# Single PSUM banks in rings of two in place of two-bank tiles, and block sums added bank by bank

## The chip, the cores and the metric

One core of a Trainium2 chip runs the whole program. The metric is device time in microseconds (us) of one execution, the median of several runs. Engines are named as in the profile: PE is TensorE's matmul stream and PEld its weight loads, DVE is VectorE, ACT is ScalarE, POOL is GpSimd, SP issues DMAs.

## The reference

Three layers follow each other. Attention with a decaying state gives `x` of 1536 tokens by 512; a gated feed-forward layer follows; then a layer of 8 experts, weighted by a normalised gate.

```
state = gamma * state + k_t v_t^T ;  y_t = scale * q_t state          # retention, 2 x 8 heads, 768 steps, dim 64
h = x @ w_in ;  g = h * clip(h + 3, 0, 6) / 6 ;  x = g @ w_out        # FFN, 512 -> 2048 -> 512
P = exp(x @ w_gate) normalised 8 times over rows and columns          # gate, 1536 x 8
out = sum over e of P[:, e] * (relu(x @ w1[e]) @ w2[e])               # 8 experts, 512 -> 1024 -> 512
```

## The kernel before

Every matmul operand is split into a high and a low part, and three products (high x high, high x low, low x high) are summed in PSUM. PSUM has eight banks, and four tags share them: `s0` and `s1` are rings of two single-bank tiles; `r` and `y` are each one tile of two banks, made once (`wide`, line 76), and `bank("r")` or `bank("y")` hands out its two halves in turn. The order of instructions on each engine is the order in which the Python code is written (a manual schedule); waits are put in by the tile framework from what reads and writes each tile. Engines take their instructions in that order.

The stages, by the time in the profiled span:

- Attention (0 to 64 us): for each of 12 chunks `attend` writes a `y` half (L326, L332), ACT and DVE copy it out as a high and a low part (L341, L342).
- FFN (64 to 366 us): `stage_a` makes `h` (L361, 12 matmuls of 512 columns, bank `s0`), and `stage_b` adds into four accumulators (L388): 0 and 1 are `s1` tiles, named acc, and 2 and 3 are the two halves of `r`. Every 4 or 6 steps a group ends: after the last three matmuls of accumulator i, `finish` copies or adds it out (ACT L403, DVE L405), then the matmuls of i + 1 follow. There are nine group ends (3 weight groups x 3 blocks of tokens).
- Experts, first half of the tokens (366 to 1004 us): a "pair" i is one block product by seven matrix products (`pair`, `product`, L668: seven times six matmuls of 384 columns, banks `s0`, `s1`), with ACT copies (L700), DVE adds (L699) and DVE and ACT relu parts (L677, L678) between. Between its steps stand pieces of `outputs`: an output tile is four pieces of three matmuls of 512 columns (L870) into one `y` half, then one eviction that scales and adds it on DVE (L877, L879, L883). Three tiles go with each pair: 36 matmuls of L870 to 42 of L668. DVE and ACT also split and combine the next weights here (L514, L515, L519 to L525). Two pairs make one turn of the outer loop.
- Experts, second half (1004 to 1446 us): pairs alternate with `outputs2`, which walks through seven products a turn (`STEPS`). Each product has two halves d (L797, six matmuls of 384 columns, one bank each) and goes into the two banks of `r` or of `y`, in the order r, y, r, y, r, r, y. After both halves DVE adds the running sum of both banks to `c` (L808, 128x768; the first four by ACT, L805). `g_forms` makes the operands (L759, L514, L515).
- Last outputs (1446 to 1469 us): L830, L837 with `r` and `y` in turn.

Of the kernel before, what the change touches and what calls it, by code (L numbers as in the profile page):

```python
# [9 lines left out]
F32 = mybir.dt.float32  # L10
# [4 lines left out]
AF = mybir.ActivationFunctionType  # L15
ALU = mybir.AluOpType
# [4 lines left out]
P = 128  # L21
# [6 lines left out]
BLK = 512  # L28
# [8 lines left out]
SB = UT // 2  # L37
# [20 lines left out]
def kernel(  # L58
# [11 lines left out]
    nc = tc.nc  # L70
# [2 lines left out]


    ps_s = ctx.enter_context(tc.tile_pool(name="ps_s", bufs=2, space=PSUM))
    wide = {t: ps_s.tile([P, 2, BLK], F32, tag=t, name=t, bufs=1) for t in "ry"}
    turn = {"r": 0, "y": 0}

    def bank(tag, name="h"):

        if tag in wide:
            turn[tag] += 1
            return wide[tag][:, (turn[tag] - 1) % 2]
        return ps_s.tile([P, BLK], F32, tag=tag, name=name)

    by_pair = lambda t: t.rearrange("p (h i) -> p h i", h=NPAIR)
    dr = ctx.enter_context(tc.tile_pool(name="dr", bufs=1, space=bass.MemoryType.DRAM))
# [153 lines left out]
    def spread(tag, to, row):  # L241

        t = by_pair(bank(tag, "dm"))
        nc.tensor.matmul(
            t.rearrange("p h i -> p (h i)"), tab[:, to * P:(to + 1) * P], tab[:, TO + row * BLK:TO + (row + 1) * BLK],
            start=True, stop=True,
        )  # L250
        return t
# [39 lines left out]
    def scores(n):  # L291
        if n >= NCH:
            return
        t = [by_pair(bank(f"s{j}", "sc")) for j in range(2)]
        for p in range(NPAIR):
            for j in range(2):
                r = slice(j * D, (j + 1) * D)
                nc.tensor.matmul(t[j][:, p], qk_t[n][r, 1, p], qk_t[n][r, 0, p], start=True, stop=True)
        for j in range(2):
            a_t[n, j] = a = at2.tile([P, NPAIR, P], F32, tag="a", name="a", bufs=4)  # L300
            nc.vector.tensor_tensor(out=a, in0=t[j], in1=dmask[:, j], op=ALU.mult)

    def state(n):
        b, c = divmod(n, NCB)
        if c == NCB - 1:
            return
        if c == 0:
            acc_r[b] = by_pair(bank("r"))
        for p in range(NPAIR):
            cs = slice(p * P, (p + 1) * P)  # L310
            nc.tensor.matmul(
                acc_r[b][:, p], ks_t[n][:, cs], kv_t[n][:, 1, cs],
                start=(c == 0 and p == 0), stop=True, skip_group_check=True,
            )
        for j in range(2):
            r = slice(j * D, (j + 1) * D)
            nc.scalar.activation(out=rs[n % 2][r, :, r], in_=acc_r[b][r, :, r], func=AF.Copy)
# [272 lines left out]
    SFIRST, SLAST = NPR // 2, NIT // 2 - 1  # L590
# [100 lines left out]
            out=slot_t[i, f, j], in0=t, scalar=0.0, in1=pb_t[e][:, j * SB:(j + 1) * SB], op0=ALU.max, op1=ALU.mult  # L691
        )

    slot_t = {}

    def pair(i):

# [88 lines left out]
    def outputs2(n, formed, fetched):  # L786
        o = y2["c"]
        seen = set()
        for k, (m, tag, fresh, q) in enumerate(STEPS):
            x = wide[tag]  # L790
            w = form_t.pop((n, m))
            hi, lo = cuts[n][k]
            for d in range(2):
                ds = slice(d * P, (d + 1) * P)
                jobs = [(w[:, s, l, ds], g[:, s]) for s in range(2) for l, g in ((0, hi), (0, lo), (1, hi))]
                for a, (l, r) in enumerate(jobs):
                    nc.tensor.matmul(  # L797
                        x[:, d, 0:SB], l, r, start=(fresh and a == 0), stop=(a == 5), skip_group_check=True
                    )
                if d == 0:  # L800
                    next(formed, None)
                    next(fetched, None)
                    yield
            if n == SFIRST and q not in seen:
                nc.scalar.activation(out=o[:, q], in_=x[:, :, 0:SB], func=AF.Copy)  # L805
                seen.add(q)
            else:
                nc.vector.tensor_tensor(out=o[:, q], in0=x[:, :, 0:SB], in1=o[:, q], op=ALU.add)  # L808
            yield

    def last_forms(n):
        for j in range(2):
# [88 lines left out]
    with tc.manual_schedule():  # L901
# [107 lines left out]
        fetched = fetch2()  # L1009
        formed = itertools.chain(*(g_forms(n) for n in range(SFIRST, SLAST)), last_forms(SLAST))  # L1010
        outs2 = itertools.chain(*(outputs2(n, formed, fetched) for n in range(SFIRST, SLAST)))
        done2 = 0

# [126 lines left out]
```

## Time and profile before

| what | us |
| --- | --- |
| median of 3 runs (1468.65 to 1476.88) | 1470.24 |
| the profiled execution's own time | 1470.33 |
| its span, first to last instruction | 1468.6 |
| PE busy / PEld busy | 1350.5 / 1198.1 |
| DVE busy | 986.2 |
| ACT busy | 529.5 |

The profiled execution is 0.1 us over the median; 1.7 us lie outside its span. PE is busy for 92% of the span, but a matmul's busy time overlaps the next one's, so what PE loses is read from its waits and from start to start. DVE's 67% is a mean over stages that differ much.

### The profile page before, as it was taken

What the parts mean: (1) busy time and instruction counts of PE and PEld (TensorE: products, weight loads), DVE (VectorE), ACT (ScalarE), POOL (GpSimd) and SP (SyncE); (2) the same over time, 40 slices, a digit from 0 to 9 for tenths busy, and PEclk for the clock granted to TensorE, in tenths of its full rate; (3) what the DMA queues carried; (4) which work ended last, traced back from release to release, by engine and by line L of the source; (5) the groups of instructions that cost most, each with busy time, mean ns of one, the idle gap of its engine ahead of it and who ended that gap; (6) DMA issues with size and microseconds to landing.
All of it is one profiled execution on the core that took longest, in us unless ns stands there. A gap on an engine that the chain in (4) does not pass through costs nothing.

```text
span 1468.6 us, 18041 instructions
## 1 busy us (share of the span) xinstructions
PE 1350.5 (92%) x7005; PEld 1198.1 (82%) x7005; DVE 986.2 (67%) x1615; ACT 529.5 (36%) x803; POOL 149.6 (10%) x223
## 2 busy tenths in 40 slices
PE   8989999998897888888888888999999999999998
PEld 7877777776776777777777777789999999999998
DVE  5866556336678766666666666566777877787773
ACT  4556434223442333333333333323323232322221
POOL 3300000000211222212222111100000000000000
PEclk8999999999999999999999999999999999999999
DMA  8522111002776677666767667759677676767661
GB/s 273 207 82 87 59 56 58 0 0 82 277 262 233 240 247 249 251 253 249 252 245 251 245 245 251 265 219 287 246 262 260 241 272 223 283 246 257 246 225 44
DMA packets 66641, 302.23 MB, mean 206 GB/s; under 512 B 7782, under 2 KB 13942, under 8 KB 58364
## 3 DMA queue, kind: packets, MB, share of 16 engines
q1 hardware_dynamic: 45020, 183.60, 35.7%
q0 software_dynamic: 21536, 117.48, 22.0%
q8 instruction: 55, 0.90, 0.2%
q14 instruction: 30, 0.25, 0.1%
HBM read 182.01 MB, written 119.04 MB: 205 GB/s over the span
## 4 chain that ended last, share of the span: by engine, by line
PE 64%; DVE 19%; ACT 8%; issue 2%; DMA 2%; POOL 0%; ACTq 0%; DVEq 0%
PE h L668 23%; PE y L870 9%; PE r L797 9%; PE h L361 8%; PE y L797 6%; PE r L388 4%; DVE o L883 4%; PE acc L388 3%; DVE w L515 3%; ACT w L514 2%; DVE st L515 2%; DVE g L678 2%; ACT st L514 2%; DMA kept<-w 1%; ACT g L677 1%
## 5 line engine op out<-in xcount | busy, mean ns | idle before, releaser
L668 PE MATMUL h<-xh,w 128*128 128x384 f32 x1792 | 528.6, 339 | 6.6 <-ACT t L700 4.8
L870 PE MATMUL y<-w,g 128*128 128x512 f32 x1152 | 316.4, 401 | 73.8 <-DVE o L883 60.5
L668 PEld LDWEIGHTS h<-xh,w 128*128 128x128 f32 x1792 | 332.0, 189 | 17.5 <-ACT t L700 5.8
L870 PEld LDWEIGHTS y<-w,g 128*128 128x128 f32 x1152 | 207.7, 189 | 132.2 <-DVE o L883 90.7
L668 PE MATMUL h<-xl,w 128*128 128x384 f32 x896 | 303.4, 339 | 0.0
L668 PEld LDWEIGHTS h<-xl,w 128*128 128x128 f32 x896 | 169.6, 189 | 9.8
L797 PE MATMUL r<-gh,w 128*128 128x384 f32 x480 | 141.4, 340 | 0.0
L514 ACT ACTIVATE gh<-g 128x768 fp32r<-128x768 f32 x64 | 54.2, 847 | 169.4 <-DVE g L759 89.8
L797 PE MATMUL y<-gh,w 128*128 128x384 f32 x360 | 106.7, 337 | 0.0
L883 DVE SCALAR_TENSOR_TENSOR o<-y,pm,o 128x512 f32<-128x512 f32 x84 | 62.6, 745 | 53.8 <-PE y L870 53.8
L797 PEld LDWEIGHTS r<-gh,w 128*128 128x128 f32 x480 | 88.2, 188 | 4.9 <-DVE c L808 4.9
L368 DVE SCALAR_TENSOR_TENSOR t<-t,h 128x512 f32<-128x512 f32 x48 | 33.0, 687 | 85.0 <-ACT t L366 84.3
L700 ACT ACTIVATE g<-h 128x384 f32<-128x384 f32 x96 | 45.1, 485 | 112.8 <-PE h L668 112.8
L515 DVE TENSOR_TENSOR w<-raw,w 128x1024 fp32r<-128x1024 f32 (+1 forms) x64 | 69.5, 1086 | 18.5 <-ACT w L514 18.5
L797 PE MATMUL r<-gl,w 128*128 128x384 f32 x240 | 80.6, 336 | 0.0
L538 POOL DMA_DIRECT2D kept<-w x32 | 17.8, 557 | 612.1 <-DVE w L515 612.1
L361 PE MATMUL h<-xhi,whi 128*128 128x512 f32 x192 | 78.5, 409 | 0.0
L361 PE MATMUL h<-xlo,whi 128*128 128x512 f32 x192 | 77.9, 406 | 0.0
L361 PE MATMUL h<-xhi,wlo 128*128 128x512 f32 x192 | 77.3, 402 | 0.3 <-DVE wlo L149 0.3
L515 DVE TENSOR_TENSOR gl<-t,gh 128x768 fp32r<-128x768 f32 x45 | 43.1, 959 | 44.4 <-ACT gh L514 44.4
L515 DVE TENSOR_TENSOR gl<-g,gh 128x768 fp32r<-128x768 f32 x64 | 60.9, 951 | 17.7 <-ACT gh L514 17.7
L366 ACT ACTIVATE t<-h,three 128x512 f32<-128x512 f32 x48 | 33.0, 687 | 92.8 <-PE h L361 91.0
(163 smaller groups left out, 2184.7 us busy)
## 6 DMA issues: line engine op xcount, KB each, us to landing
kept<-w POOLq DMA_DIRECT2D x32, 1792.0 KB, 6.3
w<-kept SPq DMA_DIRECT2D x32, 1792.0 KB, 9.3
w<-kept SPq DMA_DIRECT2D x105, 512.0 KB, 5.6
raw<-in_we SPq DMA_DIRECT2D x64, 512.0 KB, 4.2
kept<-st POOLq DMA_DIRECT2D x30, 1024.0 KB, 6.5
raw<-in_wf SPq DMA_DIRECT2D x32, 512.0 KB, 3.7
kept<-w POOLq DMA_DIRECT2D x60, 256.0 KB, 6.7
kept<-w POOLq DMA_DIRECT2D x60, 128.0 KB, 6.1
```

Source lines behind the costliest of these rows:

```text
L361: nc.tensor.matmul(h, w[:, ks], x[:, k], start=(n == 0), stop=(n == 3 * KT - 1))
L366: nc.scalar.activation(out=t, in_=h, func=AF.Relu, bias=three, scale=1.0)
L368: nc.vector.scalar_tensor_tensor(out=t, in0=t, scalar=6.0, in1=h, op0=ALU.min, op1=ALU.mult)
L388: nc.tensor.matmul(acc_b[i], l, r, start=(f == 0 and j == 0), stop=(f == nf - 1 and j == 2))
L514: nc.scalar.activation(out=hi, in_=t, func=AF.Copy)
L515: nc.vector.tensor_tensor(out=lo, in0=t, in1=f32(hi), op=ALU.subtract)
L668: nc.tensor.matmul(bank[:, 0:SB], l[:, w, ks], r[:, k], start=(start and n == 0), stop=(stop and n == 5), skip_group_check=True,)
L678: nc.vector.scalar_tensor_tensor(out=lo, in0=t, scalar=0.0, in1=f32(hi), op0=ALU.max, op1=ALU.subtract)
L700: copy = lambda out, a: nc.scalar.activation(out=out, in_=a, func=AF.Copy)
L797: nc.tensor.matmul(x[:, d, 0:SB], l, r, start=(fresh and a == 0), stop=(a == 5), skip_group_check=True)
L870: nc.tensor.matmul(acc, l[:, cs], r[:, f % 2], start=(f == 0 and k == 0), stop=(f == 3 and k == 2))
L883: nc.vector.scalar_tensor_tensor(out=o[:, tt], in0=acc, scalar=sc, in1=o[:, tt], op0=ALU.mult, op1=ALU.add)
```

## The change

`r` and `y` are no longer two-bank tiles: every `bank(tag)` call now makes a new single-bank tile from a ring of two per tag. Banks per tag stay at two, eight in all. In `outputs2` the two banks of `r` and the two of `y` are taken once, at its first turn, and each half d is added to `c` right after its own six matmuls: two DVE additions of 128x384 where one of 128x768 stood (and 8 ACT copies for 4). Matmuls, their order and all DMAs stay the same. Line numbers below the edit shift by -7 up to `pair`, -6 to -5 behind.

```diff
-    wide = {t: ps_s.tile([P, 2, BLK], F32, tag=t, name=t, bufs=1) for t in "ry"}
-    turn = {"r": 0, "y": 0}
-
-    def bank(tag, name="h"):
-
-        if tag in wide:
-            turn[tag] += 1
-            return wide[tag][:, (turn[tag] - 1) % 2]
-        return ps_s.tile([P, BLK], F32, tag=tag, name=name)
+    def bank(tag, name=None):
+        return ps_s.tile([P, BLK], F32, tag=tag, name=name or tag)
...
-            x = wide[tag]
+            if k < 2 and n == SFIRST:
+                sum_t[tag] = [bank(tag, name="acc") for d in range(2)]
+            x = sum_t[tag]
...
                     nc.tensor.matmul(
-                        x[:, d, 0:SB], l, r, start=(fresh and a == 0), stop=(a == 5), skip_group_check=True
+                        x[d][:, 0:SB], l, r, start=(fresh and a == 0), stop=(a == 5), skip_group_check=True
                     )
                 if d == 0:
                     next(formed, None)
                     next(fetched, None)
-                    yield
-            if n == SFIRST and q not in seen:
-                nc.scalar.activation(out=o[:, q], in_=x[:, :, 0:SB], func=AF.Copy)
-                seen.add(q)
-            else:
-                nc.vector.tensor_tensor(out=o[:, q], in0=x[:, :, 0:SB], in1=o[:, q], op=ALU.add)
-            yield
+                if n == SFIRST and (q, d) not in seen:
+                    nc.scalar.activation(out=o[:, q, d], in_=x[d][:, 0:SB], func=AF.Copy)
+                    seen.add((q, d))
+                else:
+                    nc.vector.tensor_tensor(out=o[:, q, d], in0=x[d][:, 0:SB], in1=o[:, q, d], op=ALU.add)
+                yield
```

Three places show what it does to the instruction streams. The first is PE in `outputs`, experts' first half, where one output tile ends and the next begins (`y_59` is the two-bank tile; an entry in brackets is the engine whose semaphore the instruction waits for). Before:

```order
L870 MATMUL y_59<-w2_5144,g_5172 128x512
L870 MATMUL y_59<-w2_5145,g_5172 128x512
L870 MATMUL y_59<-w2_5144,g_5172 128x512
L870 MATMUL y_59<-w2_5006,g_5065 128x512 [waits DVE_49]
L870 MATMUL y_59<-w2_5007,g_5065 128x512
L870 MATMUL y_59<-w2_5006,g_5065 128x512
```

The same place of the change, on PE (tiles `y_5607` and `y_5644` of the ring):

```order
L864 MATMUL y_5607<-w2_5529,g_5591 128x512
L864 MATMUL y_5607<-w2_5530,g_5591 128x512
L864 MATMUL y_5607<-w2_5529,g_5591 128x512 [waits DVE_49]
L864 MATMUL y_5644<-w2_5388,g_5374 128x512 [waits DVE_49]
L864 MATMUL y_5644<-w2_5389,g_5374 128x512
L864 MATMUL y_5644<-w2_5388,g_5374 128x512
```

Nothing moves. The wait of the next tile's first matmul was for DVE's eviction of the tile just finished, the other half of `y_59`; it is now for the eviction of the tile two back, which held the same bank. The new wait in the third row is for a low part of the operand (L671), which the earlier wait on DVE had covered.

The second place is PE at the end of a group in the FFN, the last three matmuls of accumulators 2 and 3. Before:

```order
L388 MATMUL r_58<-ghi_834,whi_696 128x512
L388 MATMUL r_58<-glo_835,whi_696 128x512
L388 MATMUL r_58<-ghi_834,wlo_697 128x512
L388 MATMUL r_58<-ghi_834,whi_696 128x512 [waits Activation_49]
L388 MATMUL r_58<-glo_835,whi_696 128x512
L388 MATMUL r_58<-ghi_834,wlo_697 128x512
```

And with the change:

```order
L381 MATMUL acc_821<-ghi_856,whi_716 128x512
L381 MATMUL acc_821<-glo_857,whi_716 128x512
L381 MATMUL acc_821<-ghi_856,wlo_717 128x512
L381 MATMUL acc_822<-ghi_856,whi_716 128x512
L381 MATMUL acc_822<-glo_857,whi_716 128x512
L381 MATMUL acc_822<-ghi_856,wlo_717 128x512
```

The wait of accumulator 3 for the eviction of accumulator 2 is gone.

The third place is DVE in `outputs2`, around one product of `STEPS`. Before:

```order
L690 SCALAR_TENSOR_TENSOR g<-h,pb 128x384
L759 TENSOR_TENSOR g<-g 128x768
L515 TENSOR_TENSOR gl<-g,gh 128x768 [waits Activation_49]
L808 TENSOR_TENSOR c<-r,c 128x768 [waits PE_49]
L759 TENSOR_TENSOR t<-g,t 128x768
```

With the change:

```order
L683 SCALAR_TENSOR_TENSOR g<-s_9361,pb 128x384
L752 TENSOR_TENSOR g<-g 128x768
L508 TENSOR_TENSOR gl<-g,gh 128x768 [waits Activation_49]
L802 TENSOR_TENSOR c<-acc,c 128x384 [waits PE_49] x2
L752 TENSOR_TENSOR t<-g,t 128x768
```

One addition has become two, each with its own wait for PE; between products with pair steps in between, the first of the two stands one step earlier in DVE's order.

## Rows read from the trace of the kernel before

**Rows 1.** Stages: length; busy PE, PEld, DVE, ACT, POOL; granted clock; DMA share, GB/s.

```profile
370.00:480.00 110.00, 93.11 (x458) 79.24 (x456) 83.44 (x194) 45.90 (x76) 23.25 (x36) 0.97 0.69 249
480.00:932.00 452.00, 393.02 (x1873) 333.51 (x1872) 305.67 (x528) 168.73 (x265) 93.15 (x144) 1.00 0.71 251
...
1004.00:1446.00 442.00, 442.00 (x2495) 436.62 (x2494) 340.08 (x471) 129.94 (x196) 0.00 (x0) 1.00 0.68 244
```

**Rows 2.** PE's waits, whole span: engine, tile, line <- releaser: us, times, longest.

```profile
PE y L870 <- DVE o L883: 60.5, 53, 1.5
```

**Rows 3.** The same for PE's weight loads.

```profile
PEld y L870 <- DVE o L883: 90.7, 78, 1.8
...
PEld r L797 <- DVE c L808: 4.9, 15, 0.3
PEld y L326 <- DVE xlo L342: 4.1, 7, 1.1
```

**Rows 4.** Who waited for tile r, whole span: us, times (L388 is the FFN).

```profile
  PEld r L388: 28.7, 9
  PE r L388: 24.9, 9
```

**Rows 5.** Timeline inside one pair, PE: start, us, what, [idle before <- releaser].

```profile
853.38 0.34 PE L668 MATMUL h<-xh,w 128*128 128x384 f32 x1
...
854.42 0.85 PE L870 MATMUL y<-w,g 128*128 128x512 f32 x3
855.11 0.34 PE L668 MATMUL h<-xh,w 128*128 128x384 f32 x1
...
857.84 0.97 PE L870 MATMUL y<-w,g 128*128 128x512 f32 x3 [0.84 <-DVE o L883]
```

**Rows 6.** The same stretch on DVE.

```profile
857.04 0.75 DVE L883 SCALAR_TENSOR_TENSOR o<-y,pm,o 128x512 f32<-128x512 f32 x1 [1.86 <-PE y L870]
```

**Rows 7.** Timeline at one group end of the FFN.

```profile
178.49 0.68 DVE L405 TENSOR_TENSOR x<-r,x 128x512 f32<-128x512 f32 x1
...
179.22 0.64 PE L388 MATMUL r<-ghi,whi 128*128 128x512 f32 x1 [3.04 <-DVE x L405]
```

**Rows 8.** Stretches at half clock, columns as in Rows 1.

```profile
363.70:370.50 6.80, 5.61 (x17) 5.33 (x18) 1.84 (x4) 0.49 (x1) 0.18 (x1) 0.50 0.98 298
sum 27.20, PE 26.01 PEld 20.30 DVE 10.58 ACT 2.10 POOL 0.18; mean PE 3.72 PEld 2.90 DVE 1.51 ACT 0.30 POOL 0.03
```

**Rows 9.** DVE's waits from 480 to 932 us.

```profile
DVE o L883 <- PE y L870: 43.3, 24, 1.9
DVE w L515 <- ACT w L514: 37.5, 48, 1.1
DVE st L515 <- ACT st L514: 28.3, 24, 1.2
DVE t L699 <- PE h L668: 21.9, 24, 0.9
DVE g L678 <- ACT g L677: 14.2, 24, 0.6
```

**Rows 10.** DVE's groups by shape, 480 to 932 us: xcount | busy, mean ns | idle before.

```profile
L515 DVE TENSOR_TENSOR w<-raw,w 128x1024 fp32r<-128x1024 f32 x24 | 29.4, 1226 | 10.4 <-ACT w L514 10.4
```

**Rows 11.** DVE's waits from 370 to 480 us.

```profile
DVE t L699 <- PE h L668: 4.9, 3, 3.2
```

**Rows 12.** DVE's groups by shape, 1004 to 1446 us.

```profile
L808 DVE TENSOR_TENSOR c<-r,c 128x768 f32<-128x768 f32 x57 | 54.5, 956 | 11.8 <-PE r L797 11.1
...
L699 DVE TENSOR_TENSOR g<-h,g 128x384 f32<-128x384 f32 x88 | 48.3, 549 | 0.2 <-PE h L668 0.2
```

**Rows 13.** DVE's waits from 1004 to 1446 us.

```profile
DVE gl L515 <- ACT gh L514: 58.5, 59, 1.6
DVE c L808 <- PE y L797: 29.3, 30, 1.7
DVE c L808 <- PE r L797: 11.1, 29, 1.2
```

More of the change, by code (lines that the diff above doesn't have):

```diff
@@ L692, in relu_scaled @@
         )
-    slot_t = {}
+    slot_t, sum_t = {}, {}
     def pair(i):
```

## The prediction

> **What bounds the kernel now.** I read the stages first. From 1004 us on PE has no idle time left: 442.0 of 442 us busy at full clock [rows 1]. Before that PE is the engine with the most work, but it waits. The view of PE's waits names the place: the first matmul of an output tile (L870) waits for DVE's eviction of an output tile (L883), 53 times, 60.5 us in all [rows 2]; its weight loads sit idle for 90.7 us for the same reason [rows 3]. The timeline says which eviction it is. At 857.84 a tile's first matmul starts after 0.84 us of idle time [rows 5], and the eviction it waited for began at 857.04, right when the tile before it was done [rows 6]: that tile lies in the other bank of `y`. PE has a second bank and doesn't use it, since both banks are one tile. The same pattern stands at each group end of the FFN. At 179.22 the matmuls of accumulator 3 start 3.04 us late, after DVE's copy of accumulator 2, the other half of `r` [rows 7]; the nine group ends cost 24.9 us of PE's and 28.7 us of its weight loads' time [rows 4]. [...]
>
> **The change, part by part.**
>
> *FFN group ends.* Accumulator 3 gets a tile of its own, so its wait for accumulator 2 goes. What is late next is the same copies, for the following group's matmuls into the same banks. PE comes to its accumulator 0 after 3 matmuls of accumulator 3 and 12 of `stage_a`, 15 x 0.23 = 3.4 us, and to accumulator 2 after 6 more, 4.8 us. In the example that counts from 179.22 - 3.04 = 176.2, so accumulator 2 is wanted at 181.0, and its copy ends at 178.49 + 0.68 = 179.2 [rows 7]; the copies of 0 and 1 stand ahead of it on DVE. The wait is hidden with about 2 us to spare. I take 26 us, between 24.9 and 28.7 [rows 4].
>
> *The clock.* Without the stalls the half-clock stretches have no cause that the trace shows. Matmuls that took 26.0 us at 0.50 take half of it at full clock [rows 8], so 13 us at most; the last stretch, 363.70 to 370.50, lies at the start of the first pair, where PE also waits for other things. I take 12; the lower bound is none.
>
> *Experts, first half, 480 to 932 us.* This is the largest term and not simply PE's wait, since another engine may take over as the limit. Two floors, over 24 pairs. PE: six matmuls of 384 columns take 1.04 us and three of 512 columns 0.69 us from start to start [rows 5], so seven products and 36 output matmuls need 7 x 1.04 + 12 x 0.69 = 15.6 us a pair, 373 us. DVE: 305.7 us busy [rows 1], and it waits 37.5 + 28.3 + 14.2 = 80.0 us for ACT results which themselves follow DVE, against 43.3 + 21.9 = 65.2 us for PE [rows 9]. Only the latter goes when PE gets faster: 452 - 65 = 386 us. A part of the ACT waits goes with it, the 10.4 us before the split of raw weights [rows 10], where ACT was held behind a copy that waited for PE: 376. So DVE's chain of 376 to 386, and not PE's 373, sets the pace; I take 380 and a gain of 72 us. The bounds are 79 (PE's floor) and half of 72, if PE and DVE, now both near full, hold each other up. Weights arrive over DMA at a share of 0.71 [rows 1]; at the new pace that is 0.85, an estimate, and DVE waits for no load in that window [rows 9].
>
> *370 to 480 us.* Here DVE also does the gate; it waits for PE only 4.9 us [rows 11], at the start, which is the FFN's last stall already counted. Whatever PE gains, DVE doesn't: nothing.
>
> *932 to 1004 us.* About 5 of the 53 waits at 1.14 us each lie here (two in each of the 24 pairs before are 48): 5 us.
>
> *Experts, second half.* The additions split. One of 128x768 takes 956 ns; the nearest row for one of 128x384 from PSUM is L699's, 549 ns [rows 12]: 2 x 549 - 956 = 142 ns more, on 101 additions (15 turns of 7 products, less the 4 that ACT copies) 14 us of DVE. What hides it is PE's 442 us: DVE is busy 340.1 us and waits 58.5 us for ACT [rows 13], with the 14 us 413. It is ahead, since it waits 29.3 + 11.1 us for PE at the additions [rows 13]; without that cover the 14 us would count in full. The second addition now ends about 0.4 us sooner after PE's last matmul, so what waits behind it gets earlier. The step r after r, 15 times 0.3 us, 4.9 us of weight-load idle time [rows 3], goes: the first bank is free before the second. I take a gain of 4; bounds -14 and +5.
>
> [...]
>
> *Attention.* The weight loads of the next chunk wait 4.1 us for the low part of the last one [rows 3]. I take 2, between 0 and 4.1.
>
> The sum: 26 + 12 + 72 + 0 + 5 + 4 + 2 = 121 us, from the profiled execution's 1470.3 us (span 1468.6 and 1.7 around it), which is 0.1 over the median: **1349 us**.
>
> **Rivals.**
>
> *PE takes back everything.* All of 28.7, 13, the 90.7 us of weight-load idle time behind L883, 5 and 4: 141 us, 1329 us. For it: PE's floor is only 1% to 3% under DVE's. Against: DVE and ACT wait for each other on every weight split, and PE can't repay that.
>
> *DVE and PE hold each other up.* Then half of the 72 comes back, the clock stretches stay where other stalls follow, and the FFN gives its 26: 26 + 4 + 36 + 5 + 4 + 2 = 77, 1393 us. For it: PE still waits for ACT copies and DVE additions inside a pair (`s0` and `s1`). Against: in the timeline PE passes from product to product inside a pair without a gap [rows 5].
>
> *It does nothing.* If the waits are really for the same bank, single tiles leave them: 1470 us. The timeline is against it, since the awaited eviction starts at the end of the tile just before, in the other half [rows 5, 6]. [...]
>
> *Slower.* The additions in the second half become what PE waits for. There are 202, each with its own wait on PE; if DVE, which works in order, came to each so late that PE stood for as long as at L883 now, 60.5 / 53 = 1.14 us [rows 2], that is 230 us, 1579 us. It decides from 121 / 202 = 0.6 us per addition. Against: DVE waits for PE there today, 40 us [rows 13], and PE for DVE only 0.3 us at one step in seven.
>
> **How the numbers follow.** Chances: forecast 0.63 (own range 1334 to 1365), everything 0.15, half 0.17, nothing 0.02, slower 0.03. The range reaches from a little under "everything" to "half" without its far end: 1324 to 1388. A measurement of this kernel can tell about 0.5% from no change, some 7 us. Faster by more: 0.63 + 0.15 + 0.17 = 0.95; within it 0.02; slower 0.03.
>
> **What the new profile would show.** Right: PE's waits hold no long entry for the output eviction or for the FFN's accumulators; the granted clock is 1.00 through the FFN; a turn of the outer loop takes about 31.7 us where it took 37.7 (452 / 12), with DVE's waits for PE nearly gone and those for ACT still there; 1004 us to the end keep their length within 10 us, and DVE shows 202 additions of near 549 ns. Wrong: a turn at 34 us or more, with PE waiting for L700's or L699's successors; half-clock stretches that stay; PE idle behind the additions in the second half.

## The result, and the profile after

The changed kernel takes **1340.5 us** (median of 4 runs, 1335.3 to 1342.5) where the kernel before takes 1471.2 us beside it: a ratio of 0.910 (0.906 to 0.914). The prediction said 1349 us. The profiled execution took 1338.8 us, its span is 1337.0.

The page's busy times and its chain of work that ended last are the first thing to read.

```profile
PE 1309.9 (98%) x7005; PEld 1196.1 (89%) x7005; DVE 988.0 (74%) x1716; ACT 524.0 (39%) x807; POOL 149.7 (11%) x223
...
PE 86%; DVE 5%; ACT 2%; issue 1%; DMA 1%; ACTq 0%; DVEq 0%
```

PE is now busy for 98% of the span, and 86% of the chain is PE's own work (a matmul's busy time overlaps the next one's: one of L864 is busy for 0.39 us on the mean, and in a row the next starts 0.23 us after it; so the 98% alone doesn't say that PE is at its floor). Of PE's waits in the whole span these are the longest, a line each for tile, line, releaser, time, number and the longest one:

```profile
PE r L464 <- DVE pm L458: 7.3, 4, 2.6
PE s L661 <- ACT t L693: 5.4, 2, 3.5
PE r L600 <- DVE pm L475: 2.1, 1, 2.1
PE s L661 <- DVE x L398: 2.0, 1, 2.0
```

The 60.5 us behind output evictions [rows 2] and the 24.9 us at the FFN's group ends [rows 4] are gone. What is left at the top is the gate (L464, L600), whose matmuls of ones wait for DVE's normalisation, and the experts' first turns (L661). The timeline of PE in a pair, where the output matmuls (L864) follow one another:

```profile
600.11 2.21 PE L864 MATMUL y<-w,g 128*128 128x512 f32 x9
602.16 0.34 PE L661 MATMUL s<-xh,w 128*128 128x384 f32 x1
...
607.35 1.53 PE L864 MATMUL y<-w,g 128*128 128x512 f32 x6
```

The six matmuls from 607.35 on are the last three of one output tile and the first three of the next, without a gap; before, 0.84 us of idle time stood at this border [rows 5]. (The nine from 600.11 on lie within one tile.) The steady stretch (twelve turns of the outer loop) and the whole of `outputs2`, as windows (length; busy PE, PEld, DVE, ACT, POOL; granted clock; DMA share, GB/s):

```profile
437.30:810.00 372.70, 372.21 (x1870) 336.53 (x1869) 301.80 (x529) 165.58 (x264) 92.93 (x144) 1.00 0.85 304
873.10:1311.10 438.00, 438.00 (x2497) 438.00 (x2496) 346.76 (x572) 129.60 (x201) 0.00 (x0) 1.00 0.70 249
```

DVE's waits in the first of the two:

```profile
DVE st L508 <- ACT st L507: 28.6, 24, 1.5
DVE w L508 <- ACT w L507: 27.1, 24, 1.1
DVE g L671 <- ACT g L670: 14.2, 24, 0.6
```

A turn, counted here and below between the evictions of its first output tile, takes 31.05 us on the mean (37.7 before). PE is busy throughout; DVE's 301.8 us and its 69.9 us of waits, now all for ACT, make 371.7 of 372.7 us as well. Both are full, and the two views alone don't tell which sets the pace. The starts in PE's timeline do: from 450 to 750 us each of its 1506 matmuls follows the one ahead by the same 0.17 us (384 columns) or 0.23 us (512 columns), never more than 0.03 us later, and on PE the turns repeat every 31.07 us (the evictions drift a little against them). PE works at its floor; how near DVE's lies, the experiments show.

Start times of the same instructions in both traces show where the 131.6 us of span come from. FFN start 62.7 became 60.9; first pair 366.3, 326.1; start of the steady turns 480.2, 437.6; their end 932.4, 810.2; first matmul of `outputs2` 1000.8, 873.1; end 1468.6, 1337.0. So, in this order: 1.7, 38.5, 2.4, 79.6, 5.5 and 3.9 us.

### The profile page after: what moved, and what is told of

Its sections match the earlier page's. It is cut to its first block, busy times and chain, and to the rows that moved or that the text cites. A ratio compares the mean times of both kernels' runs of the same rounds, so it can differ in the third digit from the quotient of the medians.

```text
span 1337.0 us, 18164 instructions
## 1 busy us (share of the span) xinstructions
PE 1309.9 (98%) x7005; PEld 1196.1 (89%) x7005; DVE 988.0 (74%) x1716; ACT 524.0 (39%) x807; POOL 149.7 (11%) x223
## 4 chain that ended last, share of the span: by engine, by line
PE 86%; DVE 5%; ACT 2%; issue 1%; DMA 1%; ACTq 0%; DVEq 0%
PE s L661 32%; PE y L864 17%; PE acc L792 17%; PE acc L381 10%; PE s L354 9%; ACT w L507 1%; DVE w L508 1%; PE r L824 1%; PE y L824 1%; DMA raw<-in_we 1%; DVE g L671 0%; ACT g L670 0%; DVE t L692 0%; DVE st L508 0%; DVE o L873 0%
## 5 line engine op out<-in xcount | busy, mean ns | idle before, releaser
L661 PE MATMUL s<-xh,w 128*128 128x384 f32 x1792 | 527.2, 338 | 9.7 <-ACT t L693 5.4
L661 PEld LDWEIGHTS s<-xh,w 128*128 128x128 f32 x1792 | 330.5, 188 | 21.6 <-ACT t L693 6.6
L661 PE MATMUL s<-xl,w 128*128 128x384 f32 x896 | 302.5, 338 | 0.1
L864 PE MATMUL y<-w,g 128*128 128x512 f32 x1152 | 300.8, 392 | 0.0
L792 PE MATMUL acc<-gh,w 128*128 128x384 f32 x840 | 244.0, 337 | 0.0
L864 PEld LDWEIGHTS y<-w,g 128*128 128x128 f32 x1152 | 214.3, 189 | 28.3
L661 PEld LDWEIGHTS s<-xl,w 128*128 128x128 f32 x896 | 168.9, 188 | 10.1 <-DVE xl L508 0.9
L792 PEld LDWEIGHTS acc<-gh,w 128*128 128x128 f32 x840 | 154.3, 188 | 0.0
L792 PE MATMUL acc<-gl,w 128*128 128x384 f32 x420 | 141.2, 336 | 0.0
L802 DVE TENSOR_TENSOR c<-acc,c 128x384 f32<-128x384 f32 x202 | 110.5, 553 | 29.2 <-PE acc L792 28.7
L693 ACT ACTIVATE g<-s 128x384 f32<-128x384 f32 x96 | 45.7, 487 | 108.7 <-PE s L661 108.7
L792 PEld LDWEIGHTS acc<-gl,w 128*128 128x128 f32 x420 | 78.9, 188 | 0.0
L354 PE MATMUL s<-xhi,whi 128*128 128x512 f32 x192 | 75.4, 392 | 0.0
```

What stands on the lines that cost most here:

```text
L354: nc.tensor.matmul(h, w[:, ks], x[:, k], start=(n == 0), stop=(n == 3 * KT - 1))
L661: nc.tensor.matmul(bank[:, 0:SB], l[:, w, ks], r[:, k], start=(start and n == 0), stop=(stop and n == 5), skip_group_check=True,)
L693: copy = lambda out, a: nc.scalar.activation(out=out, in_=a, func=AF.Copy)
L792: nc.tensor.matmul(x[d][:, 0:SB], l, r, start=(fresh and a == 0), stop=(a == 5), skip_group_check=True)
L802: nc.vector.tensor_tensor(out=o[:, q, d], in0=x[d][:, 0:SB], in1=o[:, q, d], op=ALU.add)
L864: nc.tensor.matmul(acc, l[:, cs], r[:, f % 2], start=(f == 0 and k == 0), stop=(f == 3 and k == 2))
```

## The experiments

Each run was timed beside the kernel before. The start of the FFN wandered from 55.6 to 63.4 us over all traces, in kernels whose attention differs only in the tiles of `y` and `r`, and with no order between those; where a few microseconds matter, I count from the first matmul of the FFN to the end of the span (before 1405.9, changed kernel 1276.1).

**Rings for r alone.** `y` stays a two-bank tile.

```diff
+    wide = {t: ps_s.tile([P, 2, BLK], F32, tag=t, name=t, bufs=1) for t in "y"}
...
+        if tag in wide:
+            turn[tag] += 1
+            return wide[tag][:, (turn[tag] - 1) % 2]
```

> Only the tag r is a ring of single banks (its sums in the experts' second half added bank by bank); y stays one two-bank tile, its sums added in one 128x768 addition. My theory: every y tile of a half waits for the other half's eviction, every r tile likewise, and the two are independent. Then only the FFN's group ends and its half-clock stretches go, 38.6 us by the two traces, and some of the 4 us of the second half: about 1430 us (1426 to 1436), turns of 37.7 us, FFN end near 328 us. Rival, the turns of the experts got faster because of something that r does (the gate's banks, the clock): turns fall towards 31 us and the total towards 1350 us.

Measured: 1428.7 us, ratio 0.970 (0.966 to 0.973). The FFN takes 265.5 us from its first to its last matmul's start (before 303.2, changed kernel 264.9) at a mean clock of 1.00, turns stay at 37.7 us, and `outputs2` takes 438.0 us. The waits at the evictions are all there:

```profile
PE y L874 <- DVE o L887: 60.3, 53, 1.5
```

**Rings for y alone.** The same edit with `"r"`.

> The converse: only y is a ring of single banks, r stays one two-bank tile. My theory: the FFN keeps its stalls (about 25 us of PE's waits for r) and its half-clock stretches, while the turns take 31.0 us as with the whole change; attention gives its 1.7, the turns 80 and the stretches around them 8: about 1380 us (1374 to 1388), and the gains of this run and of the r run add up to the whole 130 us. Rival, the turns are 31 us only because PE comes to them unthrottled and with single r banks for the gate: turns of 33 us or more, above 1400 us.

Measured: 1383.0 us, ratio 0.938 (0.934 to 0.942). Turns take 31.0 us, the FFN 303.5 us, `outputs2` 442.1 us. The FFN's stalls stand in PE's waits as before:

```profile
PE r L387 <- DVE x L404: 18.4, 6, 4.3
PE r L387 <- ACT x L402: 7.4, 3, 4.0
```

The two gains, 44.4 and 90.0 us against 1473.0, add up to 134; the whole change gave 131. The tags act apart, as the sum of the prediction has it.

**The additions alone.** Both tags stay two-bank tiles; only the additions are split, each right behind its own half.

```diff
+    wide = {t: ps_s.tile([P, 2, BLK], F32, tag=t, name=t, bufs=1) for t in "ry"}
...
+                sum_t[tag] = [wide[tag][:, d] if tag in wide else bank(tag, name="acc") for d in range(2)]
```

> Both tags stay two-bank tiles; only the additions of the second half are split, each 128x384 half right after its own six matmuls, 202 for 101. My theory: the work of the split, 14 us of DVE, lies under PE; but each half's addition now holds the whole tile, and the second half's matmuls wait for it. A product of the pair, 1.04 us, usually stands between, which covers the addition's 0.55 us and the way to it unless DVE is late: 1470 to 1490 us. Rival 1, the additions bank by bank are themselves part of the gain: 1466 us or less. Rival 2, the slower case of the prediction: PE stands 0.6 us or more at each of 101 first halves, 1530 us or more.

Measured: 1571.6 us, ratio 1.068 (1.063 to 1.073): slower by 98.6 us, and my theory for this run was wrong; the second rival came true. From the FFN's first matmul to `outputs2` it takes 935.5 us (938.1 before); `outputs2` takes 545.4 us in place of 441.9. PE's waits in it, and the stage as a window, here and in the kernel before:

```profile
PE r L798 <- DVE c L808: 57.8, 42, 2.8
PE y L798 <- DVE c L808: 11.5, 15, 1.2
```

```profile
998.40:1543.80 545.40, 475.51 (x2497) 452.44 (x2496) 354.21 (x573) 131.72 (x201) 0.00 (x0) 0.96 0.57 200
```

```profile
1000.80:1442.70 441.90, 441.90 (x2497) 437.04 (x2496) 340.09 (x472) 130.32 (x197) 0.00 (x0) 1.00 0.69 247
```

PE stands idle for 69.9 us, and its busy time grew by 33.6, part of it since the clock is not at its full level all through this stage (mean 0.96, with 1.00 before and in the changed kernel): twelve stretches of 3.4 us, 41 us in sum, run at a granted 0.50. In the FFN of the kernel before, matmuls of 512 columns started every 0.43 us in such stretches and every 0.23 us outside them. The timeline of PE shows one place:

```profile
1253.63 0.34 PE L667 MATMUL s<-xh,w 128*128 128x384 f32 x1
1254.69 0.44 PE L798 MATMUL r<-gh,w 128*128 128x384 f32 x1 [0.72 <-DVE c L808]
```

And DVE's, of the same place:

```profile
1253.21 0.96 DVE L514 TENSOR_TENSOR gl<-t,gh 128x768 fp32r<-128x768 f32 x1 [0.94 <-ACT gh L513]
1254.08 0.55 DVE L808 TENSOR_TENSOR c<-r,c 128x384 f32<-128x384 f32 x1
```

I had priced the way to the addition and its 0.55 us against the pair product of 1.04 us that covers them. What was missing is DVE's queue: the addition stands behind a subtraction of 0.96 us that first waits 0.94 us for ACT. With two-bank tiles the second half's matmuls wait for all of that. This is the mechanism of the prediction's slower case, at 57 places of 1.2 us; in the changed kernel, where a bank is not wanted back before a product later, it has no hold: PE is busy for 438.0 of 438.0 us.

**Rings, additions late.** The changed kernel with both additions behind the second half.

```diff
+                if d == 0:
+                    yield
+                    continue
+                for e in range(2):
...
+                        nc.vector.tensor_tensor(out=o[:, q, e], in0=x[e][:, 0:SB], in1=o[:, q, e], op=ALU.add)
```

> The whole change except the place of the additions: single banks in rings for both tags, but both 128x384 additions of a product stand behind its second half, as the one wide addition did. My theory: where they stand hardly matters, since PE comes back to a bank of r or y a product later; 1340 us within 4, the second half 438 us long. Rival, it is the early first addition that keeps r free for the product after it (r follows r once a turn, r follows y follows r otherwise): 0.3 us at 15 places at least, 1345 us, and up to 0.5 us at each of 101, 1390 us.

Measured: 1335.4 us, ratio 0.907 (0.904 to 0.910), 0.6 us under the expected 1336 to 1344 and not the rival's 1345 or 1390. `outputs2` takes 438.0 us, as in the changed kernel, and from the FFN's first matmul on the kernel takes 1275.7 us (1276.1). The early addition bank by bank gives nothing; with single tiles one just can't add both banks in one instruction.

**One more DVE instruction.** Each pair of the first half writes one low part twice.

```diff
+        if f == j == 0:
+            nc.vector.scalar_tensor_tensor(out=lo, in0=t, scalar=0.0, in1=f32(hi), op0=ALU.max, op1=ALU.subtract)
```

> The changed kernel with one more DVE instruction in each pair of the first half: the low part of one hidden block (128x384, 0.56 us) is written a second time, same values. It asks what holds a turn at 31.0 us. Theory A, DVE's chain with its waits for ACT is as full as PE (301.8 us busy and 70 us of waits in 372.7): a turn becomes 32.1 us, the total 1340 + 16 x 1.1 = about 1357 us. Theory B, PE alone sets 31.0 us and DVE waits for ACT because it has time: turns stay at 31.0 to 31.2 us, and only the first two turns, where DVE sets the pace, grow: 1340 to 1344 us.

Measured: 1351.9 us, ratio 0.918 (0.915 to 0.921); turns of 31.9 us, 0.9 more for two instructions of 0.56 us, each of which overlaps its neighbour by some 0.08 us. Theory A, though 5 us under its 1357: there is next to no room in DVE's chain.

**Less for PE.** The changed kernel without the third product of the first half's output tiles.

```diff
-                for k, (l, r) in enumerate(((ghi, whi), (ghi, wlo), (glo, whi))):
+                for k, (l, r) in enumerate(((ghi, whi), (glo, whi))):
```

> The changed kernel with the third of the three products (high x low weight) left out of the first half's output tiles, so part of the computation is missing: 24 instead of 36 matmuls of 512 columns a pair. PE's floor of a turn falls from 31.0 to 25.5 us. It measures DVE's own floor, which the prediction put at 376 to 386 us for 12 turns, 31.3 to 32.2 us a turn. Theory A: DVE's chain is really there, near 31 us: turns of 30 to 31 us, 1325 to 1340 us. Theory B: DVE's floor lies far lower, since its waits for ACT shrink when it is pressed: turns near 26 us, about 1340 - 14 x 5 = 1270 us.

Measured: 1331.2 us, ratio 0.904 (0.902 to 0.907). Turns take 31.00 us, although PE has 12 matmuls in each pair less to do. PE's waits between 450 and 750 us are now inside the pair; below them the same stretch as a window:

```profile
PE s L661 <- DVE t L692: 23.6, 19, 1.2
PE s L661 <- ACT t L693: 12.9, 39, 0.5
```

```profile
450.00:750.00 300.00, 263.25 (x1278) 224.01 (x1276) 242.97 (x425) 133.87 (x213) 74.69 (x117) 1.00 0.85 304
```

DVE's 243.0 us and its 56.1 us of waits for ACT fill the window, and PE has time left. So the floor of DVE's chain is 31.00 us a turn, 0.07 under PE's.

**ACT's copies one piece ahead.** The pieces of the weight jobs are reordered, so that a copy of a high part and the subtraction that needs it are apart.

```diff
-        parts(w[:, 0, S1:], w[:, 1, S1:], t)
+        subs = high(w[:, 0, S1:], w[:, 1, S1:], t)
+        yield True
+        subs()
```

> The changed kernel with ACT's copies of the weights' high parts put one step ahead of DVE's subtractions that need them (another DVE instruction of the same job between them), for the raw and the combined weights; work and number of instructions stay. DVE's waits for these copies (8.7 + 7.0 us from 326 to 437 us, 55 us in the steady turns) should shrink to little. In the steady turns nothing comes of it if PE sets 31.0 us; before them, where DVE is the bound, the turns before 437 us get shorter by most of those 15.7 us: about 1327 us (1322 to 1333). Rival: ACT is in order too, its copies come no earlier, the waits move to other places: 1338 us or more.

Measured: 1343.2 us, ratio 0.912 (0.908 to 0.915), no gain. DVE's waits stay where they were (25.9 and 27.4 us between 440 and 800 us). In the profiled execution, the slowest of its four, the kernel takes 1283.7 us from the FFN's first matmul on, 7.6 more than the changed kernel; nearly all of them fall before the steady turns, and I have no cause for them. A step of the pair takes two pieces, so for the combined weights copy and subtraction ended up in the same step with nothing in between. There the edit didn't do what it was to test, so this run decides nothing on the theory.

**The gate spread over two turns.**

```diff
-                    if it and at % 2 == 0:
+                    if it and at % 4 == 0:
```

> The changed kernel with the gate's 16 steps spread over two turns (every fourth step of a pair in place of every second). In the changed kernel PE waits 9.5 us in one turn, of 43.7 us, for gate results of DVE (the chain row sums, reciprocal, product, matmul of ones). With twice the distance those waits go, and half of the gate's DVE work moves to a turn which has PE's 31.0 us as its bound. If PE's waits are the cost: about 1332 us (1329 to 1336). Rival, the gate's DVE work is what counts and DVE is full in both turns: 1338 to 1342 us.

Measured: 1345.7 us, ratio 0.914 (0.911 to 0.916). The first four turns take 33.7, 37.0, 38.8 and 37.3 us, in sum 4.6 more than in the changed kernel. PE's waits for the gate are out of the list between 326 and 800 us, but those inside the pair (for L692 and L693) have grown from 5.9 to 18.9 us. The forecast missed, and the time lies above the rival's 1338 to 1342 too: without the gate's waits nothing is gained, which is the rival's point, but why it costs something no run shows.

**Copies a whole step ahead.** Two pieces of sums are joined, and two yields or an addition between yields stand before the subtraction (shown for the combined weights of the first layer; three more copies are moved in a like way).

```diff
-        parts(w[:, 0, S1:], w[:, 1, S1:], t)
+        subs = high(w[:, 0, S1:], w[:, 1, S1:], t)
+        yield True
+        yield True
+        subs()
```

> The changed kernel with the weight jobs in another order: ACT's copies of the high parts a whole step of the pair ahead of DVE's subtractions, so that an addition and an eviction, some 1.2 us, or an addition of 0.5 us, lie between them. In the run that put them only one job piece ahead the two pieces fell into the same step and DVE's waits for the combined weights (25.9 and 27.4 us) stayed. Now about 0.6 us of 1.13 and 0.9 of 1.77 (both waits of the st step) should go in each pair, 3 us a turn. With DVE's chain freed, PE's floor of 31.0 us stays in the steady turns, and the two turns before them, where DVE sets the pace (36.5 and 43.7 us), lose about 3 us each: 1334 us (1330 to 1338). Rival, the subtractions' waits move to the relu parts behind the copies in ACT's order: no gain, 1340 us.

Measured: **1330.1 us**, ratio 0.903 (0.901 to 0.906), the lowest median of the versions that compute everything (the interval of the late additions overlaps it). Between 450 and 750 us the longest of DVE's waits are:

```profile
DVE st L512 <- ACT st L511: 14.5, 20, 1.0
DVE o L896 <- PE y L883: 13.7, 19, 0.7
DVE t L711 <- PE s L680: 11.4, 19, 0.9
DVE g L690 <- ACT g L689: 9.6, 19, 0.5
```

DVE waits for PE again: it has time left, and PE holds the steady turns at 31.07 us. The first three turns took 36.2, 37.7 and 29.2 us (36.5, 43.7 and 31.0 in the changed kernel), so not about 3 us each in the first two, as expected, but 0.3 and 6.0. From the FFN's first matmul on it takes 1269.9 us, 6.2 less.

**The same with less for PE.**

> The same order with the third product of the output tiles left out (part of the computation is missing): PE's floor is 25.5 us a turn, so the turn shows DVE's. If the waits for ACT are part of what holds DVE at 31.0 us, turns fall to about 28 us and the total to about 1331 - 13 x 3 = 1292 us (1285 to 1300). Rival, something other than this chain holds 31.0 us (loads, or the pace of the program): turns stay at 31.0 us, 1325 us or more.

Measured: 1283.9 us, ratio 0.871 (0.868 to 0.874), 1 us under the expected range; turns of 27.5 us. The window and DVE's waits in it:

```profile
450.00:750.00 300.00, 298.72 (x1443) 251.80 (x1442) 273.79 (x481) 148.69 (x241) 83.42 (x129) 1.00 0.95 345
```

```profile
DVE st L512 <- ACT st L511: 15.6, 22, 0.7
DVE g L690 <- ACT g L689: 9.1, 22, 0.4
```

273.8 and 24.7 us make 298.5 of 300: DVE's chain again, 3.5 us a turn shorter. PE's 298.7 us look as full, but 168 of its matmuls start up to 0.2 us later after the one ahead than their usual 0.17 or 0.23 us, 19.4 us in sum (none in the run with the copies a step ahead and all products), and such a delay hardly shows as idle time (1.3 us in the window), since a matmul's busy time, 0.34 or 0.39 us in the changed kernel, covers most of it. DVE's waits for ACT were part of its floor, and nothing else, loads included, holds 31.0 us.

**The same with the gate spread.**

> The order with copies a step ahead and the gate spread over two turns as well. Alone, spreading gave nothing: its first four turns took 33.7, 37.0, 38.8 and 37.3 us, 146.8 in sum where the changed kernel has 142.2, since DVE was full in each. With 3 us of DVE's time free in every turn the gate's share of each turn is half hidden: first four turns near 137 us, total 1329 us (1324 to 1335). Rival, the gate's chain itself is long in every step it shares with the pair: the sum of the four turns stays above 142 us and the total at 1340 us.

Measured: 1335.0 us, ratio 0.906 (0.903 to 0.909), the upper end of the forecast. The first four turns take 137.2 us in sum, as expected, but 134.2 without the spreading: 3 us worse in the two profiled executions, not better, and the intervals of the two ratios overlap.

## Why the prediction was right, and where it was off

*The reading of the waits.* The prediction took the waits at L870 and at the FFN's group ends for waits for the other bank of the same tile. The runs with one tag each show it: each tag takes its own waits away, and only those. The two banks of `y`, used in turn, let matmuls and eviction overlap only after each had a tile of its own: 60.5 us of waits before, none after. *It does nothing* falls with that.

*FFN and clock*: 26 + 12 predicted, 38.5 measured, and nearly the same in the run with rings for r. The half-clock stretches of the FFN went with the stalls: of the seven before, 27.2 us in sum [rows 8], six began 0.1 to 1.1 us after PE had stood for 2.7 to 4.0 us and one while it stood for 3.4 us, and with rings for r the FFN has a mean clock of 1.00. The whole stage in the changed kernel, and the two short stretches at 0.50 that remain behind it, where turns are still held up (PE stood for 3.5 us until 341.4, at L661, and for 2.4 us until 401.4, at L464):

```profile
60.90:326.10 265.20, 264.68 (x1178) 216.91 (x1177) 164.55 (x283) 130.12 (x179) 0.72 (x1) 1.00 0.17 56
...
341.40:344.80 3.40, 3.38 (x11) 3.38 (x12) 2.97 (x6) 1.60 (x3) 0.79 (x1) 0.50 0.64 243
402.90:406.30 3.40, 3.40 (x10) 2.73 (x9) 2.23 (x5) 1.06 (x1) 0.00 (x0) 0.50 0.92 281
```

How the 38.5 divide into stalls and clock no run separates.

*Experts, first half, steady turns*: 72 predicted, 79.6 measured; this is the term that was mis-sized, and most of the 10.6 us by which the sum fell short (121 for 131.6). The step that failed was "DVE's chain of 376 to 386, and not PE's 373, sets the pace; I take 380". The runs put DVE's floor at 12 x 31.00 = 372 us (less for PE: 31.00) and PE's at 12 x 31.07 = 373 (copies a step ahead: DVE has room, and 31.07 stay). The changed kernel's turns repeat every 31.07 us on PE, none of whose matmuls there starts late, so PE sets the pace, by 0.07 us a turn. The prediction had PE's floor right and DVE's too high. The subtraction that gave 376 was right in kind: the 65.2 us of waits for PE went, and the 10.4 us before the split of raw weights [rows 10] became 1.1:

```profile
L508 DVE TENSOR_TENSOR w<-raw,w 128x1024 fp32r<-128x1024 f32 x24 | 29.4, 1226 | 1.1
```

The rest is DVE's busy time, 305.7 to 301.8 us, though no instruction got shorter. One that follows another without a wait starts some 0.08 us before the other's end, and with fewer waits more of them do so. The two traces settle it: in both, the durations of DVE's instructions in the twelve turns add up to 337.3 us; before, 384 of them start ahead of their neighbour's end, 31.6 us in sum, and in the changed kernel 431, 35.6 us. I had then taken a middle value, 380, where only the lower end had a reason.

*PE takes back everything* is the rival that comes nearest in the steady turns: they run at PE's floor, the forecast's upper bound of 79. Its total of 141 us is too high, mainly since it counts the 90.7 us for which the weight loads sat idle behind L883; PE got back 79.6 + 5.5 = 85.1 us there.

*DVE and PE hold each other up* does not happen in the steady turns, though it had its ground: both engines' floors lie within 0.07 us, and one instruction more on DVE in each pair lengthens the turn by 0.9 us.

*370 to 480 us*: nothing predicted, 2.4 measured. DVE is the bound there, as said: a third less of PE's output work doesn't shorten these turns (35.4 and 44.2 us for 36.5 and 43.7), and neither does the distance of the gate's steps, but the copies a step ahead do.

*932 to 1004 us*: 5 predicted, 5.5 measured.

*Second half*: 4 predicted, 3.9 measured, all of it from r (438.0 us with rings for r alone, 442.1 for y alone). The group of split additions, on DVE between 873.1 and 1311.1 us:

```profile
L802 DVE TENSOR_TENSOR c<-acc,c 128x384 f32<-128x384 f32 x200 | 109.5, 553 | 29.2 <-PE acc L792 28.7
```

553 ns each, against 549 taken; a split costs 2 x 553 - 956 = 150 ns by these rows, where the prediction took 142. PE is busy for 438.0 of 438.0 us, so the added DVE work lies under it. That the second addition "ends about 0.4 us sooner after PE's last matmul, so what waits behind it gets earlier" was worth nothing, as the late additions show. The slower rival's mechanism is real: with two-bank tiles the split additions cost 98.6 us. The prediction weighed the additions and the rings as one; it never asked what the additions would do without the rings.

*Attention*: 2 predicted, 1.7 measured, which is inside the wandering of that stage and shows nothing.

## What to carry to other kernels

Two banks of one tile used in turn may not be two buffers (here they cost 60.5 and 24.9 us of PE's waits): where a matmul into one half waits for the eviction of the other, give each bank a tile of its own before anything else is tuned. Splitting an instruction so that each half follows its own work cost PE nothing where each half had its own tile; on the shared tiles it made PE's next half wait for what stood ahead of the other's reader in DVE's queue, 57 times and 69.3 us in all. When a wait goes, work out the floors of all engines in the same stretch, and where two come out within some per cent, treat the lower bound of the one in front as likely as its middle.

## What the runs showed of the hardware

On DVE an instruction that follows without a wait starts before the one ahead has ended by the records (599.92 + 0.55 us, next start 600.39), so the same work shows as less busy time where waits are fewer (1.3% in the steady turns, where the durations add up to the same 337.3 us). And the clock fell in a stage that had not shown it: in `outputs2` with the additions alone, with 57 stalls of PE of 1.2 us on average in 545 us, the mean granted clock is 0.96, with twelve stretches of 3.4 us at 0.50, where the kernels before and after keep 1.00.
